# The first token group's output products in the seven-product scheme: a fused HGRN2 attention and maxout FFN kernel

## The chip, the cores and the metric
One core of one Trainium2 chip. The metric is the device time of one execution in microseconds (us); the median of three runs of the kernel before is 415.52 us (415.25 to 416.81). Beside the times there is one profiled execution, from which every duration below is taken.

## What is computed
An HGRN2 recurrence gives x, and a maxout FFN with three input matrices is applied to it, all in float32:

```python
f = 1 / (1 + exp(-f_logit))                       # q, k, v, f_logit: (4, 8, 768, 48)
for t in range(S):                                # S = 768
    state = f[:, :, t, :, None] * state + einsum('bhd,bhe->bhde', k[:, :, t], v[:, :, t])
    y[:, :, t] = einsum('bhd,bhde->bhe', q[:, :, t], state)
x = y.transpose(0, 2, 1, 3).reshape(3072, 384)
h = maximum(maximum(x @ w1, x @ w2), x @ w3)      # w1, w2, w3: 384 x 768
out = h @ w_out                                   # w_out: 768 x 384
```

## The kernel before, in words
**Units and groups.** The work is cut into 24 units (u = 0 to 23) of 128 tokens, which go through the recurrence, and into 6 groups (g = 0 to 5) of 4 units, which go through the FFN as blocks of 512 tokens. For a unit the program runs `sigmoids` (ACT), `scan` (DVE, L329), `after` (DVE turns k; GpSimd writes `ends` L339 and `kh` L340), `before` (DVE scan L347; GpSimd writes `qh` L351), `carry` (GpSimd, L357), `keys_by_blocks` (DVE transposes of `kh`, L382), `pairs` (PE, L392; it needs the unit's `kh` and `qh`), `values` and `sums` (PE, L411 and L436), and `finish` (PE L500, then three ACT copies L506 into xT). In the code `pack` then moves the rows of xT that lie in the wrong place, by two DMAs (L519). Units 0 to 5 are loaded by rows; from unit 6 (`BY_ROWS`) one `load` fetches two units by 24 DMAs (L183).

**The FFN.** The maximum is taken over differences: w1 is subtracted from w2 and w3 (`apart`, L745), the maximum with 0 of the two remaining products gives hm, and the part `x @ w1 @ w_out` is added back through a precomputed matrix `w_nat = w1 @ w_out` (`linear`, L772, nine matmul steps in three rows `a`). `place` (L450) rearranges w2 - w1, w3 - w1 and `w_nat` by ten DMAs each into `placed[0]`, `placed[1]` and `w_lin`, the order in which groups 1 to 5 hold x.

- Group 0 has a path of its own, `ffn_first` (L786): plain products (L537), rounding of the float64-typed weights as they arrive (`round_to`, L750), `linear`, and `outputs` (L557): for each of its four units nine matmuls of 128x384 into one bank, an ACT copy to `o`, and two stores.
- Groups 1 to 5 use a Strassen-like scheme of seven block products in place of eight. `inputs_by_pairs` (L858) makes hm; it needs sums of the weights (`mix_in`, L833, four GpSimd operations of 128x768 into `w_sum` and `placed[1]`) and of x (`sums_of_x`, L845, five GpSimd operations). `outputs_by_pairs` (L614) makes the outputs by matmuls of 128x192; it needs sums of hm (`sums_of_hm`, L605, four GpSimd operations of 128x256 for each of three j pairs) and differences of w_out and `w_lin` (`mix` L583, `mix_x` L589, on GpSimd). One PSUM bank `a` accumulates in several stages: after each stage ACT copies it out (`read`, L635) and the next product adds into the same bank.

**Order.** All engines' instructions run in program order (`manual_schedule`). The FFN is a Python generator that yields an estimated PE cost after each piece. The main loop (L1060) runs the steps of a unit and between them calls `fill(part)` (L956), which adds `part` to a budget and draws FFN pieces while the budget is above zero. With `part` = 2360 for u = 4 to 7 and 2432 after that, the program fixes which FFN piece stands between which unit steps, and `PART` (L976) is such that four units draw just the estimated cost of one group of the new scheme. The cost of the yields of one group therefore shifts every later FFN piece against the unit steps. `ffn(g)` is appended in the loop of unit 4g + 4, after `pack(3, 3)` of the group.

**Queues around the change.** SP issues loads, `place`, `pack` and stores one by one, about 0.63 us each. In program order it has: `load(8)` (24 DMAs, in the loop of u = 5), `v` of unit 7, `place` for `placed[0]`, `v` of unit 8, `place` for `placed[1]`, `place` for `w_lin`, `pack(0, 2)` of group 1, `load(10)`. GpSimd has, after the last rounded weight piece (L258): kh and qh of unit 7, its `carry`, the four `mix_in` with kh and qh of unit 8 between them, one `mix`, the steps of unit 9, `sums_of_x(1)`, and the other three `mix`. The buffers: `w_mix` lies in `w_in[2]`, `w_sum` in `placed[2]`, `s_mix` (sums of hm) in `w_in[1]`.

Of the kernel before, what the change touches and what calls it, by code (L numbers as in the profile page):

```python
# [55 lines left out]
def kernel(  # L56
# [33 lines left out]
    def fast():  # L90
        ctx = ExitStack()
        with ctx:
# [463 lines left out]

            def outputs(hm, xT, i):  # L557
                p = bank()
                t = slice(i % 2 * UT, (i % 2 + 1) * UT)
                terms = [(hm[:, j, i * UT:(i + 1) * UT], w_out[:, j, :]) for j in range(NJ)]  # L560
                terms += [(by_halves(xT)[:, i // 2, k, t], w_nat[:, k, :]) for k in range(NK)]
                for n, (lhsT, rhs) in enumerate(terms):
                    nc.tensor.matmul(p[:, 0:DM], lhsT=lhsT, rhs=rhs, start=(n == 0), stop=(n == NJ + NK - 1))  # L563
                    if n % NK == NK - 1:
                        if n == NJ + NK - 1:
                            o = o_four[:, i]
                            nc.scalar.copy(o, p[:, 0:DM])
                            store(i, o)
                        yield NK * DM * COLUMN

            HJ, HD = NJ // 2, DM // 2
            corner = lambda k, n: w_out[:, k::2, n * HD:(n + 1) * HD]
            w_mix = [corner(0, 1)] + [w_in[2][:, :, n * HD:(n + 1) * HD] for n in range(4)]
            x_mix = [w_lin[:, 0, HD:]] + [w_mix[4][:, n] for n in range(2)] + [keep.tile([128, HD], FP32, name="mix")]
# [4 lines left out]
            def mix(n):  # L583

                dst, x, y = ((w_mix[2], corner(1, 1), corner(0, 1)), (w_mix[0], corner(0, 1), corner(0, 0)),
                             (w_mix[1], corner(1, 1), w_mix[0]), (w_mix[3], corner(1, 0), w_mix[1]))[n]
                nc.gpsimd.tensor_tensor(dst, x, y, op=ALU.subtract)

# [16 lines left out]
            def sums_of_hm(hm, jj):  # L605
                sums_of_pair(hm[:, 2 * jj], hm[:, 2 * jj + 1], *(t[:, jj] for t in s_mix))
# [7 lines left out]
            def outputs_by_pairs(g, hm, xT):  # L614
                tile_of = lambda p, n: slice((2 * p + n) * UT, (2 * p + n + 1) * UT)
                half = lambda n: slice(n * HD, (n + 1) * HD)
                order = [*range(HJ - 1), HJ, HJ - 1]
                A = lambda k, n: lambda p: [(xT[:, k] if jj == HJ else hm[:, 2 * jj + k])[:, tile_of(p, n)] for jj in order]
# [3 lines left out]
                              for t, x in zip(s_mix, s_of_x(xT)))  # L622
                X = lambda n: lambda p: [xT[:, 2, tile_of(p, n)]]
                lin, lin_mix = [[w_lin[:, 2, half(n)]] for n in range(2)], [w_mix[4][:, 2]]
                partial = [w_nat[:, n, :] for n in range(NK)]
                last = g == NU // GRP - 1
# [16 lines left out]
                a, b, c = bank(), bank(True), bank(True)  # L643
                sums_of_x_pair(xT, 0)
                into(b, 0, X(0), lin[0])
# [4 lines left out]
                for p in range(2):  # L650
                    into(a, p, A(0, 0), C(0, 0), early)
                    if p:
                        sums_of_x_pair(xT, 1)
                    yield COST - PART_COST
                    into(b, p, A(1, 0), C(1, 0), early)
                    yield COST - PART_COST
# [129 lines left out]
            def ffn_first(xT):  # L786
# [4 lines left out]
                for j, t in steps:  # L791
                    w = t.stop - t.start
                    for i in (1, 2):
                        p = yield from product(xT, j, i, t)
                        if i == 1:
                            nc.scalar.copy(hm[:, j, t], p)
                        else:
                            nc.vector.scalar_tensor_tensor(hm[:, j, t], hm[:, j, t], 0.0, p, op0=ALU.max, op1=ALU.max)
                        round_to(ROUNDED[n_step])
                        load_weights(2, rounded[0] - 1)  # L800
                        yield (1 if w == TOK else NK) * w * COLUMN
                        n_step += 1
                        if n_step in TURNED:
                            yield from turn(TURNED[n_step])
                for a in range(NK):
                    if a < 2:
                        for n in range(2 * NK + 2):
                            place(placed[a].bitcast(FP32), w_in[a + 1], n)
                    for cost in linear(a):
                        round_to(rounded[0] + 1)  # L810
                        yield cost
                for n in range(2 * NK + 2):
                    place(w_lin, w_nat, n)
                made = iter([lambda n=n: mix_in(n) for n in range(4)] + [lambda: mix(0)])
                for i in range(GRP):
                    for n, cost in enumerate(outputs(hm, xT, i)):
                        if i or n:
                            next(made, lambda: None)()
                        if i == GRP - 1 and n == 1 and 1 in packed:
                            sums_of_x(1)  # L820
                        if i == GRP - 1 and n == 2:
                            for k in range(1, 4):
                                mix(k)
                        yield cost

# [4 lines left out]
            w_two = [t.bitcast(FP32) for t in placed[0:2]]  # L830
            w_sum = [placed[2].bitcast(FP32)[:, n] for n in range(NK)]

# [25 lines left out]
            def inputs_by_pairs(g, hm, xT):  # L858
# [57 lines left out]
                def fourth(n):  # L916
# [5 lines left out]
                    sums_of_hm(hm, n)  # L922
                    if g == 1:
                        for i in ((0, 1), (2, 3, 4), ())[n]:
                            mix_x(i)
                    yield COST
# [54 lines left out]
            with tc.manual_schedule():  # L981
# [78 lines left out]
                for u in range(GRP, NU):  # L1060
# [7 lines left out]
                    if u > GRP:  # L1068
                        finish(u - 1, xT)
                        if u % GRP == 3:  # L1070
                            pack(0, 2, xT)
                        elif u % GRP == 0:
                            pack(3, 3, xT)
                    if u % GRP == 0:
# [6 lines left out]
                    if u + 2 <= BY_ROWS:  # L1081
                        load(u + 2)
                    if BY_ROWS <= u + 3 < NU and u % 2:
                        load(u + 3, one, "fkq" if u % GRP == 1 else "f")
                    if u + 2 < NU:
                        load_v(u + 2)
                    keys_by_blocks(u, 3)
                    if n < NU:
                        if n < BY_ROWS:
                            sigmoids(n)  # L1090
                        if n != BY_ROWS:
                            scan(n)
# [6 lines left out]
                    if BY_ROWS < u + 2 < NU and u % GRP == 0:  # L1099
                        load(u + 2, one, "k")  # L1100
                    values(u)
                    if n < NU:
                        carry(n)
# [8 lines left out]
                    if u + 2 >= CHECKS:  # L1112
                        check_load(u + 2 - CHECKS)
                    if BY_ROWS <= u + 2 < NU:
                        sigmoids(u + 2)
# [272 lines left out]
```

## Time and profile before

| what | value |
|---|---|
| median of three runs | 415.52 us |
| the profiled execution's own time | 416.47 us |
| its span, first to last instruction | 414.6 us |
| TensorE (PE) busy | 397.8 us, 96% |
| GpSimd (POOL) busy | 245.2 us, 59% |
| VectorE (DVE) / ScalarE (ACT) busy | 290.8 us, 70% / 178.7 us, 43% |
| mean granted TensorE clock | 0.998 |
| PE: `linear` | 77.28 to 91.83 us |
| PE: `outputs` of group 0 | 91.83 to 120.12 us |
| PE: first product of groups 1, 2, 3, 4 | 120.12, 181.64, 241.26, 300.86 us |

A float32 matmul stands as two records in the trace, so the 36 matmuls of `outputs` are 72 records. The duration of a record contains the pipeline's depth; the pace is the distance from one start to the next. A line of the timeline gives the start, the duration, the engine, the line of the kernel, output and inputs, and, in brackets, the idle time before it with what ended it.

### The profile page before, as it was taken

Reading aid. Unit: us, or ns where it says so; the run is one execution under the profiler, and the core shown is the slowest. Engines: PE = TensorE matmul, PEld = TensorE weight load, DVE = VectorE, ACT = ScalarE, POOL = GpSimd, SP = SyncE. Lnnn points to the kernel's source line nnn. Section 1 sums busy time; section 2 is a strip of 40 time slices with the busy share of each in tenths; the row PEclk is TensorE's granted clock in tenths of the full one; section 3 lists DMA queues with packets and bytes.
Section 4 is the critical chain, followed back from the end, with each engine's and each line's share of the span. In section 5 each row is a group of like instructions: output and inputs, shape, how many; then the busy total and the mean of one; then the engine's idle time right before and its main releaser. Section 6 shows DMA issues by size and latency. Waiting matters only on the chain.

```text
span 414.6 us, 11546 instructions
## 1 busy us (share of the span) xinstructions
PE 397.8 (96%) x4598; PEld 332.4 (80%) x4598; DVE 290.8 (70%) x569; ACT 178.7 (43%) x412; POOL 245.2 (59%) x270
## 2 busy tenths in 40 slices
PE   4988999999999999999999999999999999999995
PEld 4766775566668889998889988889988899988984
DVE  6987897996695899898888976988894550002500
ACT  2478786511223531444541354533345324576210
POOL 2189694730989887487496376667466860435700
PEclk9999999999999999999999999999999999999999
DMA  8989987677356767377625376724473011541002
GB/s 170 237 261 273 250 231 93 86 143 159 83 104 96 122 114 132 70 118 89 137 78 104 52 117 86 163 64 80 71 146 96 2 55 44 148 136 60 0 21 62
DMA packets 181562, 47.21 MB, mean 114 GB/s; under 512 B 160448, under 2 KB 179200, under 8 KB 181504
## 3 DMA queue, kind: packets, MB, share of 16 engines
q1 hardware_dynamic: 178032, 45.62, 54.0%
q10 hardware_dynamic: 3472, 0.81, 0.9%
q8 instruction: 37, 0.61, 0.6%
q14 instruction: 21, 0.17, 0.1%
HBM read 37.75 MB, written 4.72 MB: 102 GB/s over the span
## 4 chain that ended last, share of the span: by engine, by line
PE 76%; DVE 6%; SPq 5%; POOL 3%; DMA 3%; ACT 3%; issue 2%; ACTq 0%; POOLq 0%; DVEq 0%
PE p L870 16%; PE p L631 14%; PE tr L870 13%; PE tr L631 11%; PE p L537 6%; PE p L563 3%; PE y L411 3%; PE y L500 2%; PE p L776 2%; SPq L174 2%; DMA raw<-in_moe_w_dram 2%; PE a L392 2%; PE y L436 2%; DVE ks L382 2%; SPq L164 1%
## 5 line engine op out<-in xcount | busy, mean ns | idle before, releaser
L382 DVE STREAM_TRANSPOSE ks<-kh 32x128 f32<-32x128 f32 x256 | 77.4, 302 | 11.9 <-POOL kh L340 7.7
L870 PE MATMUL tr<-xT,placed 128*128 128x256 f32 x300 | 72.6, 385 | 0.3 <-DVE hm L913 0.3
L870 PEld LDWEIGHTS tr<-xT,placed 128*128 128x128 f32 x300 | 55.7, 190 | 9.3 <-ACT hm L878 1.2
L870 PE MATMUL p<-xT,placed 128*128 128x256 f32 x180 | 45.1, 382 | 0.3 <-POOL xT L854 0.3
L339 POOL COPY ends<-r 128x8 f32<-128x8 f32 x24 | 9.8, 407 | 48.5 <-DVE r L329 48.5
L870 PEld LDWEIGHTS p<-xT,placed 128*128 128x128 f32 x180 | 33.7, 190 | 5.3 <-POOL xT L854 0.7
L537 PE MATMUL p<-xT,w_in 128*128 128x256 f32 (+1 forms) x108 | 33.9, 458 | 3.0 <-POOL w_in L745 2.2
L329 DVE TENSOR_TENSOR_SCAN r<-gate,from_one 128x520 f32<-128x520 f32 x24 | 31.5, 1314 | 6.1 <-ACT gate L308 3.0
L340 POOL TENSOR_TENSOR kh<-kt,r 128x512 f32<-128x512 f32 x18 | 30.1, 1671 | 7.6 <-DVE kt L296 6.2
L639 DVE TENSOR_TENSOR o<-tr,w_in 128x384 f32<-128x384 f32 (+1 forms) x11 | 5.7, 521 | 38.6 <-PE tr L631 35.1
L347 DVE TENSOR_TENSOR_SCAN prod<-gate,from_inv 128x520 f32<-128x520 f32 x24 | 32.1, 1336 | 0.0
L603 POOL TENSOR_TENSOR w_in<-hm 128x256 f32<-128x256 f32 x15 | 11.1, 739 | 34.9 <-DVE hm L921 32.2
L506 ACT COPY xT<-y 64x256 f32<-64x256 f32 (+1 forms) x60 | 22.1, 369 | 19.2 <-PE y L500 18.1
L870 PE MATMUL p<-w_in,placed 128*128 128x256 f32 x120 | 30.0, 379 | 0.0
L913 DVE TENSOR_TENSOR hm<-tr,hm 128x512 f32<-128x512 f32 x15 | 10.3, 688 | 26.6 <-PE tr L870 19.7
L537 PEld LDWEIGHTS p<-xT,w_in 128*128 128x128 f32 x108 | 19.5, 190 | 11.8 <-issue 6.0
L636 ACT COPY w_in<-p 128x384 f32<-128x384 f32 x15 | 7.2, 478 | 46.0 <-PE p L631 46.0
L631 PE MATMUL p<-w_in,hm 128*128 128x192 f32 x120 | 25.4, 335 | 1.1 <-ACT w_in L636 1.1
L258 POOL TENSOR_TENSOR w_in<-top_bits,rest_bits 128x384 uint32<-128x384 uint32 x18 | 21.8, 1218 | 7.6 <-DVE top_bits L252 4.7
L280 ACT ACTIVATE raw<-top_bits 128x384 f32<-128x384 f32 x48 | 25.2, 526 | 0.4
L870 PEld LDWEIGHTS p<-w_in,placed 128*128 128x128 f32 x120 | 22.8, 190 | 3.1
L631 PE MATMUL tr<-w_out,w_in 128*128 128x192 f32 x120 | 24.4, 326 | 0.0
(159 smaller groups left out, 907.6 us busy)
## 6 DMA issues: line engine op xcount, KB each, us to landing
raw<-in_moe_w_dram SPq DMA_DIRECT2D x24, 384.0 KB, 3.8
v_ld<-in_v_dram SPq DMA_DIRECT2D x48, 96.0 KB, 3.2
placed<-in_moe_w_dram SPq DMA_DIRECT2D x12, 384.0 KB, 5.4
out_dram<-o SPq DMA_DIRECT2D x46, 96.0 KB, 2.2
placed<-in_moe_w_out_dram SPq DMA_DIRECT2D x6, 384.0 KB, 6.3
f_ld<-in_f_logit_dram SPq DMA_DIRECT2D x36, 64.0 KB, 3.4
k_ld<-in_k_dram SPq DMA_DIRECT2D x36, 64.0 KB, 2.5
q_ld<-in_q_dram SPq DMA_DIRECT2D x36, 64.0 KB, 2.5
```

The costliest lines, as they stand in the source:

```text
L258: nc.gpsimd.tensor_tensor(dst, by(top), by(rest), op=ALU.add)
L280: nc.scalar.activation(over, size, AF.Relu, scale=(-1 / HI_MIN, 1.0)[step - 1], bias=(1.0, -HI_END * (1 - 2.0 ** -24))[step - 1], accum_ou ...
L329: nc.vector.tensor_tensor_scan(r[:, 0:LEN][:, ::-1], flat(gate)[:, ::-1], flat(from_one)[:, ::-1], 1.0, op0=ALU.mult, op1=ALU.max)
L340: (nc.vector if u < BY_ROWS else nc.gpsimd).tensor_tensor(kh.rearrange("p h a t -> p a h t"), kt, by_batch(r[:, 1:LEN + 1].rearrange("p (x ...
L347: nc.vector.tensor_tensor_scan(flat(prod), flat(gate_tiles[u % 2]), flat(from_inv[u % 2]), 1.0, op0=ALU.mult, op1=ALU.max)
L382: nc.vector.transpose(ks[n * 32:(n + 1) * 32, :, par, e0:e0 + 32], kh[p0:p0 + 32, :, a, t0:t0 + 32])
L411: nc.tensor.matmul(y[o:o + DP, a, hp * C:(hp + 1) * C], lhsT=v_ld[s, 2 * hp + par, :], rhs=d["at"][s, par, hp, :], start=(hp == 0), stop=F ...
L506: nc.scalar.copy(xT[o, :, t0 + a * C:t0 + (a + 1) * C], y[i, a, 0:HP * C].rearrange("p (h t) -> p h t", h=HP))
L537: nc.tensor.matmul(p if w < TOK else p.rearrange("p (two t) -> p two t", two=2), lhsT=w_in[i][:, kt, j * 128:(j + 1) * 128], rhs=x[:, t.st ...
L563: nc.tensor.matmul(p[:, 0:DM], lhsT=lhsT, rhs=rhs, start=(n == 0), stop=(n == NJ + NK - 1))
L631: nc.tensor.matmul(b[:, p * HD:(p + 1) * HD], lhsT=x, rhs=w, start=id(b) not in begun, stop=True, skip_group_check=True)
L870: nc.tensor.matmul(b[:, j * HALF:(j + 1) * HALF], lhsT=w[:, (2 * n + j) * 128:(2 * n + j + 1) * 128], rhs=x, start=begin and j == 0, stop= ...
```

## The change
`ffn_first` now calls `outputs_by_pairs(0, hm, xT)` in place of four `outputs`. For group 0 (`mixed` false) x is not part of the seven-product scheme: it enters through plain products with `w_nat`, three matmuls for each half where the later groups have one, and `order` has three entries instead of four. Partial sums go to `rests` instead of `w_nat`.

Other steps move. Both `place` calls for the input weights stand ahead of `linear`, and `load(8)` moves from the loop of u = 5 to that of u = 6, in two parts (f after `pairs`, k and q after `values`), with `sigmoids(8)` moved to the loop of u = 7. `mix(0)` to `mix(2)` stand in `linear`'s first row, the twelve operations of `sums_of_hm` in its second, `mix(3)` and the new `mix(4)` behind it, the four `mix_in` with the first four pieces of the outputs, `mix_x` behind them. `w_mix` and `w_sum` trade places in memory. The stores of group 0 come later, out of `store_late` in group 1. `pack` of group 1 goes to ACT's queue.

```diff
-            w_mix = [corner(0, 1)] + [w_in[2][:, :, n * HD:(n + 1) * HD] for n in range(4)]
+            spare = placed[2].bitcast(FP32).rearrange("q k c -> q (k c)")
+            w_mix = [corner(0, 1)] + [spare[:, n * NK * HD:(n + 1) * NK * HD].rearrange("q (k c) -> q k c", k=NK)
+                                      for n in range(4)]
...
-                dst, x, y = ((w_mix[2], corner(1, 1), corner(0, 1)), (w_mix[0], corner(0, 1), corner(0, 0)),
-                             (w_mix[1], corner(1, 1), w_mix[0]), (w_mix[3], corner(1, 0), w_mix[1]))[n]
-                nc.gpsimd.tensor_tensor(dst, x, y, op=ALU.subtract)
+                dst, x, y = ((w_mix[2], corner(1, 1), corner(0, 1)), (w_mix[1], w_mix[2], corner(0, 0)),
+                             (w_mix[3], corner(1, 0), w_mix[1]), (w_mix[0], corner(0, 1), corner(0, 0)),
+                             (w_mix[4], w_nat[:, :, 0:HD], w_nat[:, :, HD:]))[n]
+                nc.gpsimd.tensor_tensor(dst, x, y, op=ALU.add if n == 1 else ALU.subtract)
...
-                order = [*range(HJ - 1), HJ, HJ - 1]
+                mixed = g > 0
+                order = [*range(HJ - 1), *[HJ] * mixed, HJ - 1]
...
+                else:
+                    X = lambda n: lambda p: [by_halves(xT)[:, p, k, n * UT:(n + 1) * UT] for k in range(NK)]
+                    lin = [[w_nat[:, k, half(n)] for k in range(NK)] for n in range(2)]
+                    lin_mix = [w_mix[4][:, k] for k in range(NK)]
+                    partial = [rests[:, 0], rests[:, 1], rests[:, 0]]
...
+                for a in range(2):
+                    for n in range(2 * NK + 2):
+                        place(placed[a].bitcast(FP32), w_in[a + 1], n)
                 for a in range(NK):
-                    if a < 2:
-                        for n in range(2 * NK + 2):
-                            place(placed[a].bitcast(FP32), w_in[a + 1], n)
-                    for cost in linear(a):
-                        round_to(rounded[0] + 1)
+                    for n, cost in enumerate(linear(a)):
+                        round_to(len(pieces))
+                        if a == 0:
+                            mix(n)
+                        elif a == 1:
+                            sums_of_hm(hm, n)
                         yield cost
                 for n in range(2 * NK + 2):
                     place(w_lin, w_nat, n)
-                made = iter([lambda n=n: mix_in(n) for n in range(4)] + [lambda: mix(0)])
-                for i in range(GRP):
-                    for n, cost in enumerate(outputs(hm, xT, i)):
...
+                mix(3)
+                mix(4)
+                for n, cost in enumerate(outputs_by_pairs(0, hm, xT)):
+                    if n < 4:
+                        mix_in(n)
+                    yield cost
+                for m in range(5):
+                    mix_x(m)
...
-            w_sum = [placed[2].bitcast(FP32)[:, n] for n in range(NK)]
+            w_sum = [w_in[2][:, n] for n in range(NK)]
...
-                    if g == 1:
-                        for i in ((0, 1), (2, 3, 4), ())[n]:
-                            mix_x(i)
...
+                        queues = act if u <= 2 * GRP else one
...
-                            pack(0, 2, xT)
+                            pack(0, 2, xT, queues)
                         elif u % GRP == 0:
-                            pack(3, 3, xT)
+                            pack(3, 3, xT, queues)
...
-                    if BY_ROWS <= u + 3 < NU and u % 2:
-                        load(u + 3, one, "fkq" if u % GRP == 1 else "f")
-                    if u + 2 < NU:
+                    if u == BY_ROWS:
+                        load(u + 2, one, "f")
+                    elif u + 1 != BY_ROWS:
+                        if BY_ROWS <= u + 3 < NU and u % 2:
+                            load(u + 3, one, "fkq" if u % GRP == 1 else "f")
+                    if u + 2 < NU and u != BY_ROWS:
                         load_v(u + 2)
...
-                        if n < BY_ROWS:
+                        if n < BY_ROWS or n == BY_ROWS + 2:
                             sigmoids(n)
...
+                    if u == BY_ROWS:
+                        load(u + 2, one, "kq")
+                        load_v(u + 2)
...
-                    if BY_ROWS <= u + 2 < NU:
+                    if BY_ROWS <= u + 2 < NU and u != BY_ROWS:
                         sigmoids(u + 2)
```

## The prediction
> **What bounds the kernel now.** I read the page first: PE is busy 397.8 of 414.6 us, at full clock in all slices but for the start.
>
> ```profile
> PE 397.8 (96%) x4598; PEld 332.4 (80%) x4598; DVE 290.8 (70%) x569; ACT 178.7 (43%) x412; POOL 245.2 (59%) x270
> ...
> PE   4988999999999999999999999999999999999995
> ...
> POOL 2189694730989887487496376667466860435700
> ```
>
> From 77 us on PE hardly stops, so the end moves by the PE work that goes, less each gap that comes. The second view is PE's timeline: where do gaps arise? At the very end, where no unit steps are left, ACT's copy of bank `a` stands open between two products into that bank. First the end of group 5's second stage, then the same place in group 1:
>
> ```profile
> 398.39 0.49 PE L631 MATMUL p<-w_in,w_in 128*128 128x192 f32 x2
> 399.44 0.92 PE L631 MATMUL p<-w_in,hm 128*128 128x192 f32 x4 [0.57 <-ACT w_in L636]
> ...
> 168.80 0.49 PE L631 MATMUL p<-w_in,w_in 128*128 128x192 f32 x2
> 169.22 0.66 PE L500 MATMUL y<-qh,state 48*48 48x64 f32 x32
> 169.81 0.69 PE L392 MATMUL a<-qh,kh 48*64 48x64 f32 x32
> 170.44 0.92 PE L631 MATMUL p<-w_in,hm 128*128 128x192 f32 x4
> ```
>
> Two records issue in 0.325, so at 398.39 the next could start at 398.72; it starts at 399.44: **0.72 us lost**. At 168.80 the same copy costs nothing, as `finish` and `pairs` of a unit stand in between. The third view is GpSimd's timeline around group 0's outputs (PE 91.83 to 120.12):
>
> ```profile
> 81.02 1.00 POOL L258 TENSOR_TENSOR w_out<-top_bits,rest_bits 128x384 uint32<-128x384 uint32 x1 [0.88 <-DVE top_bits L254]
> ...
> 87.18 1.96 POOL L340 TENSOR_TENSOR kh<-kt,r 128x512 f32<-128x512 f32 x1 [0.71 <-DVE kt L296]
> ...
> 104.15 1.81 POOL L839 TENSOR_TENSOR placed<-placed 128x768 f32<-128x768 f32 x1 [13.09 <-DMA w_in<-w_in]
> ...
> 106.06 1.19 POOL L340 TENSOR_TENSOR kh<-kt,r 128x512 f32<-128x512 f32 x1
> 107.21 1.18 POOL L351 TENSOR_TENSOR qh<-qt,prod 128x512 f32<-128x512 f32 x1
> ...
> 114.45 2.34 POOL L587 TENSOR_TENSOR w_in<-w_out 128x576 f32<-128x576 f32 x1
> ...
> 128.83 1.41 POOL L587 TENSOR_TENSOR w_in<-w_out 128x576 f32<-128x576 f32 x1
> ```
>
> GpSimd idles 13.09 us for `place`'s DMAs, and qh of unit 8 ends at 108.39, just ahead of its `pairs` on PE at 108.49. The same operation takes 1.19 or 1.96, and 1.41 or 2.34: the long ones lie over a DVE scan (prod from 86.96, r from 113.86). A scan costs GpSimd about 0.8.
>
> **The change part by part.** The terms are against this execution (416.47 us, span 414.6), 0.95 above the median; I carry their sum to 415.52.
>
> *1. PE work of group 0.* Before: 36 matmuls of 384 columns, 72 records; six undisturbed ones (96.96 to 98.89) give 0.322 each, 23.2 us. After: eleven stages of six 192-column matmuls, 66 or 132 records at 0.1625 (20 in 3.25 in the chain of waits), 21.45; smaller pieces add some 0.1. Saved 1.8 to 2.6 (the upper by L563's whole stretches, 24.0); I take **-1.9**, since restarts after unit steps are nearly as many.
> The Trainium skill, "TensorE: Matmul & The Clock Gate", Back-to-back issue gap, gives N/2.4 + 2.5 ns for an isolated matmul. As an estimate with two passes a record that is 0.325 and 0.165, and the saving 1.6: the rule charges short matmuls more than the rows do.
>
> *2. GpSimd's queue from 82.02 us.* After the last L258 (ends 82.02) the program now has, without a gap: `mix` 0 to 2, one `sums_of_hm`, ends, kh, qh of unit 7, two `sums_of_hm`, `carry`, **`mix(3)`**, `mix(4)`, four `mix_in`, ends, kh, **qh of unit 8**. From start to start uncontended: mix 1.4 to 1.45, four sums 2.85 (L603, 141.37 to 144.22), ends+kh+qh 2.45, carry 0.78, mix_in 1.79. So: 82.0 + 4.35 + 2.85 + 2.45 + 5.7 + 0.8 = 98.15, `mix(3)` to 99.6, `mix(4)` to 101.0, `mix_in` to 108.1, qh(8) to 110.6 at the earliest. Under this unbroken queue lie DVE's scans r(7), prod(7) (84.97, 86.96 now), r(8), prod(8): three by `mix(3)`, four by qh(8), +2.4 and +3.2. I take 102.0 and 113.8.
> "GPSIMD Engine Reference", section 3.1 of the Trainium skill, puts a two-input operation at 2.6 cycles of 1.2 GHz per element. As an estimate the queue's 11,456 elements are 24.8 us, qh(8) would end at 106.9 and the second wait below vanish. That lacks each operation's start and the scans; the rows decide.
>
> PE's demand: lin ends at 91.83; two stages 1.95, finish and pairs (7) and a restart to 94.92 as now; then six pieces of 0.65 to **98.9**, where the first seven-product stage (`c`, s1 by `w_mix[0]`) needs `mix(3)`: wait 102.0 - 98.9 = **+3.1** (0.7 without scans). On to `pairs(8)`: 0.975, values 1.08, 2.05, 0.975, the uncovered copy of `a` (below) **+0.7**, three pieces 2.9, finish 0.5: 9.1 in all, 111.1; qh(8) is there at 113.9: **+2.8** (1.9 without scans). Behind the waiting matmuls stands all of PE's queue; DVE and ACT wait for PE later, so nothing is won beside. Sum for group 0: -1.9 + 3.1 + 0.7 + 2.8 = +4.7.
>
> *3. Queues.* `place` (20 x 0.63) starts on SP where `load(8)` started: 72.2, its last lands near 87, long before `mix_in`. `load(8)` then issues 84.9 to 90 (f) and to 99.4 (k, q), landing near 102; DVE turns q(8) at 101.6 now, and qh(8) is stuck in GpSimd's queue until 112: covered; if GpSimd were early, at most 1 us. `pack` passes to ACT: two issues of 0.70 (L519 on ACT, 349.27) ahead of sig(8), which ends near 98 where DVE is still on unit 7's transposes: nothing. Eight stores leave SP's stretch of 117 to 134, so k, q of unit 10 and x of group 1 come earlier. Now DVE waits 3.5 and 1.5 for them, GpSimd 1.9 for `pack`. PE's stretch of group 1 is 61.5 (120.12 to 181.64) against 59.6 for groups 2 and 3, so at most 1.9 returns, at least nothing as GpSimd comes late; I take **-1.4**. The removed `mix` and `mix_x` of group 1 lie in the same 1.9.
>
> *4. The shifted budget.* Group 0's yields fall from 23.04 to 21.12 us, so by the program's own sums every later FFN piece stands 1.92 earlier among the unit steps. I went through the budget yield by yield; for the present kernel this gives the timeline's order. In the new order the second stage's copy and the next product into `a` come in one `fill` in groups 0 to 4; `finish` and `pairs` come only after that product. ACT's copy (0.48 and two semaphores) then stands open: 0.72 each in groups 1 to 4 and the 0.7 above. The third copy loses `values` as cover: 0.08 (403.45 to 403.53 in group 5), about 0.5 in group 4 where ACT has `pack` and checks ahead of it. In return `sixth` and `fifth` part (-0.09 a group). Three times 0.71 and once 1.13: **+3.3**. The x sums on DVE come as close as 0.4 us ahead of their matmul; bound 0 to 0.3 a group, I take 0.
>
> Total: 4.7 - 1.4 + 3.3 = **+6.6**, 415.5 + 6.6 = **422.1 us**. Its own bounds: no scan contention, all 1.9 back, group 4 without the 0.5: -1.9 + 0.7 + 0.7 + 1.9 - 1.9 + 2.8 = +2.3, 417.8; nothing back, scans at 0.95, x sums late: +9.7, 425.2.
>
> **The rivals.**
> *GpSimd keeps up* (the other side: not slower). If `w_mix[0]` is there by 98.9 and qh(8) by 108.0, both waits go. For: 13 us of idle time lie in this stretch now. Against: the bare minimum of the rows is already 99.6 and 110.6. Price: -1.9 + 0.7 - 1.4 + 3.3 = +0.7, 416.2.
> *The copies stay covered.* If unit steps stand between copy and product, 0.7 and 3.3 go: -1.9 + 3.1 + 2.8 - 1.4 = +2.6, 418.1. Against: the budget decides, and a yield of 1.28 against a balance of 0.83 is not close.
> *Both*, and the change does just what it is arranged for: -1.9 - 1.4 = -3.3, 412.2.
> *It doesn't begin as early as it says*: if `mix(3)`, in place in w_out, holds up all products with w_out behind it and not `w_mix[0]` alone, PE waits at 95.1 already; 102.0 + 13 = 115 against 113.9 at `pairs(8)`: +1.1, 423.2. Nothing in the trace tells.
>
> **How the numbers follow.** Forecast 0.55, GpSimd keeps up 0.13, copies covered 0.10, both 0.14, earlier wait 0.08. A measurement tells 0.5% (2.1 us) from no change. Faster by more: 0.14 (both). Same: 0.13 of keeping up less 0.02 for its upper end, and 0.04 of copies covered: 0.15. Slower: 0.71. The range leaves out "both" and a little above 425: 414.5 to 425.2.
>
> **What would show it.** PE: gaps ahead of L631 put down to POOL L587 near 99 and ahead of L392 to POOL L351 near 111; one gap of 0.6 to 0.7 at each group's A01 product put down to ACT L636; group starts shifted by +4.7, then 0.7 a group. GpSimd: no idle time from 82 to 113. It is wrong if group 1 starts before 120 us, or if `finish` stands between copy and product.

## The result and the profile after

The changed kernel takes **427.52 us** (median of 4 runs, 426.21 to 429.69), the kernel before in the same series 415.88 (415.25 to 416.81): ratio 1.028 [1.0235, 1.0332], slower by some 11.6 us. The forecast was 422.1 with a range up to 425.2: the direction held, the size did not. The profiled execution took 426.21 us with a span of 424.3.

From the page of the changed kernel, PE's share, its slices and its clock:

```profile
PE 399.3 (94%) x4658; PEld 342.3 (81%) x4658; DVE 295.4 (70%) x571; ACT 179.0 (42%) x413; POOL 254.5 (60%) x284
...
PE   4988999997699999999999999999999999999995
...
PEclk9999999998899999999999999999999999999999
```

The two weak slices of PE, 7 and 6, are 95 to 117 us; there the clock drops as well, which it does in no slice of before:

```profile
PEclk9999999999999999999999999999999999999999
```

So I cut PE's timeline of each kernel at the first product of the linear stage and at the first product of each group (us):

| stretch | before | changed | e1 | e3 | e9 |
|---|---|---|---|---|---|
| linear stage and group 0's outputs | 42.84 | 51.52 | 47.87 | 47.93 | 42.08 |
| group 1's stretch | 61.52 | 60.49 | 60.46 | 59.50 | 59.72 |
| group 2's | 59.62 | 60.48 | 60.47 | 59.61 | 59.62 |
| group 3's | 59.60 | 60.47 | 60.46 | 59.62 | 59.61 |
| group 4's | 57.81 | 58.60 | 58.70 | 57.82 | 57.81 |
| group 5's, to the end of the span | 55.93 | 55.95 | 56.1 | 57.1 | 56.0 |

(e1, e3, e9 are experiments below; e3's last stretch has 1.1 us more behind the last product, where the last stores land.) Group 0 pays 8.7 us in the profiled execution, the fastest of the four; forecast was 4.7. Group 1 wins 1.0 in all; groups 2 to 4 pay 0.8 to 0.9 each. PE's timeline of the changed kernel has these gaps in group 0 (start, duration, engine, line, operation; in brackets the idle time ahead and who ended it):

```profile
101.03 1.97 PE L623 MATMUL tr<-w_out,w_in 128*128 128x192 f32 x6 [2.23 <-POOL w_out L572]
...
108.61 3.69 PE L623 MATMUL p<-placed,w_in 128*128 128x192 f32 x12 [2.55 <-ACT rest_bits L628]
112.87 2.22 PE L623 MATMUL p<-placed,hm 128*128 128x192 f32 x12 [0.57 <-ACT rest_bits L628]
...
117.09 0.67 PE L500 MATMUL y<-qh,state 48*48 48x64 f32 x32 [1.03 <-DVE st L444]
```

The first is the forecast wait for `mix(3)`, the third the uncovered copy of `a`. The second and the fourth are new. The fourth is late by the same cause as the second: `st` stands on DVE behind the turning of q(8), which waits 2.20 us for q of unit 8 to land. At 108.61 PE waits for `read(a, 0)`, an ACT copy of 0.46 us. Why is it late? ACT's timeline:

```profile
95.08 1.40 ACTq L519 DMA_DIRECT2D xT<-xT  x2
107.56 0.63 ACT L311 ACTIVATE sig<-f_ld 128x512 f32<-128x512 f32 x1 [12.12 <-DMA f_ld<-in_f_logit_dram]
108.10 0.46 ACT L628 COPY rest_bits<-p 128x384 f32<-128x384 f32 x1
```

The copy stands behind sig(8), and sig(8) waits 12.12 us for unit 8's f. SP issues that load only at 99.78. SP's timeline:

```profile
79.83 19.85 SPq L461 DMA_DIRECT2D placed<-w_in  x8
99.78 4.29 SPq L183 DMA_DIRECT2D f_ld<-in_f_logit_dram  x8
```

Eight issues of `place` take 19.85 us, since one stands. In before the same eight took 5.04:

```profile
96.84 5.04 SPq L461 DMA_DIRECT2D placed<-w_in  x8
```

SP's waits of the changed kernel in the same stretch (us in total, times, longest):

```profile
SPq L461 <- DMA xT<-xT: 13.8, 1, 13.8
```

`xT<-xT` is the `pack(0, 2)` that this kernel issues on ACT. Why should a `place` wait for it? In the built program every DMA of SP and of ACT reports its landing on one of eight completion semaphores, taken in turn by both queues, and waits first for the DMA that used that number before. SP's ten DMAs of the second `place`, with the number that each takes:

```
L454 placed<-w_in  DMAHW4
L454 placed<-w_in  DMAHW7
L461 placed<-w_in  DMAHW0, 1, 2, 3, 4
L461 placed<-w_in  DMAHW5
L461 placed<-w_in  DMAHW6
L461 placed<-w_in  DMAHW7
```

Between the first and the second, `pack(0, 2)` took 5 and 6. So the eighth and ninth wait until it has landed, and it waits for ACT's copies (94.30) of what PE's `finish(6)` gives at 93.6. SP's order is strict, and all of unit 8's loads stand behind. The Trainium skill, "DMA: Bandwidth & Descriptors", section "Why a DMA increments its semaphore by 16 and not by 1", says why such a wait has to be there: two DMAs in flight on one semaphore can't be told apart. In this trace the wait takes 13.8 us of SP.

### The profile page after: what moved, and what is told of

Its sections match the earlier page's. It is cut to its first block, busy times and chain, and to the rows that moved or that the text cites. A ratio compares the mean times of both kernels' runs of the same rounds, so it can differ in the third digit from the quotient of the medians.

```text
span 424.3 us, 11681 instructions
## 1 busy us (share of the span) xinstructions
PE 399.3 (94%) x4658; PEld 342.3 (81%) x4658; DVE 295.4 (70%) x571; ACT 179.0 (42%) x413; POOL 254.5 (60%) x284
## 4 chain that ended last, share of the span: by engine, by line
PE 82%; SPq 4%; DVE 3%; issue 2%; DMA 2%; POOL 2%; ACT 2%; ACTq 0%; DVEq 0%; POOLq 0%
PE p L864 19%; PE tr L864 16%; PE p L623 16%; PE tr L623 12%; PE p L537 5%; SPq L183 3%; PE y L500 3%; PE y L411 3%; PE a L392 2%; PE p L769 2%; PE y L436 2%; SPq L461 1%; POOL w_in L258 1%; PE y L407 1%; PE tr L291 1%
## 5 line engine op out<-in xcount | busy, mean ns | idle before, releaser
L864 PE MATMUL tr<-xT,placed 128*128 128x256 f32 x180 | 43.7, 379 | 0.0
L864 PEld LDWEIGHTS tr<-xT,placed 128*128 128x128 f32 x180 | 34.2, 190 | 4.6
L623 PE MATMUL p<-placed,hm 128*128 128x192 f32 x144 | 30.9, 337 | 4.1 <-ACT w_in L628 3.6
L623 PE MATMUL tr<-w_out,w_in 128*128 128x192 f32 x144 | 29.7, 334 | 2.2 <-POOL w_out L572 2.2
L864 PE MATMUL tr<-xT,w_in 128*128 128x256 f32 x120 | 31.7, 387 | 0.0
L685 POOL TENSOR_TENSOR o<-top_bits,w_in 128x384 f32<-128x384 f32 x5 | 5.1, 1016 | 43.5 <-ACT w_in L628 43.5
L864 PE MATMUL p<-xT,placed 128*128 128x256 f32 x120 | 29.6, 383 | 0.0
L623 PEld LDWEIGHTS p<-placed,hm 128*128 128x128 f32 x144 | 23.6, 190 | 7.3 <-ACT w_in L628 6.2
L623 PEld LDWEIGHTS tr<-w_out,w_in 128*128 128x128 f32 x144 | 24.7, 193 | 2.6 <-POOL w_out L572 2.5
L588 POOL TENSOR_TENSOR w_in<-hm 128x256 f32<-128x256 f32 x18 | 14.0, 780 | 21.0 <-DVE hm L915 21.0
```

The source lines that it names most:

```text
L588: engine.tensor_tensor(dst, x, y, op=op)
L623: nc.tensor.matmul(b[:, p * HD:(p + 1) * HD], lhsT=x, rhs=w, start=id(b) not in begun, stop=True, skip_group_check=True)
L864: nc.tensor.matmul(b[:, j * HALF:(j + 1) * HALF], lhsT=w[:, (2 * n + j) * 128:(2 * n + j + 1) * 128], rhs=x, start=begin and j == 0, stop= ...
```

## The experiments

Theory after the result: (a) that wait of SP costs what group 0 has above its forecast; (b) the rest is as forecast, GpSimd's queue and the uncovered copies, and behind each long gap a slow clock comes on top. Rivals: ScalarE itself is what `pack` delays; the slow clock is an independent cost; the shift harms by late inputs, not by copies.

**e1: both packs back on SP**, the changed kernel otherwise.

```diff
-                        queues = act if u <= 2 * GRP else one
+                        queues = one
```

> Group 1's two pack steps go back from ACT's queue to SP's; all else is the changed kernel. Theory 1 (ordering between the two DMA queues): the trace of the changed kernel shows SP stuck for 13.8 us in the second place (84.1 to 97.9), put down to the landing of pack's DMA, which ACT issues after PE's finish of unit 6. With pack on SP that wait goes; unit 8's f is issued near 85 to 90 instead of 99.8 to 104, ACT's sig(8) ends near 98 instead of 108.2, and PE's wait ahead of the second-stage product (2.55 us, read put down to ACT) goes. What stays: the wait for mix(3) near 99 (2 to 3 us), slow records after it, and about 0.7 us at the copy of bank a in each group. Sum: 3 to 5 us faster than the changed kernel, 422 to 425 us. Rival A (place waits for its buffers: the raw weights or the differences in w_in): the 14 us gap in place stays and the time stays at 427. Rival B (GpSimd's queue alone sets group 0): the gap goes, but qh of unit 8 is late all the same, and the time falls by less than 1.5 us.

422.82 us (422.52 to 423.45), ratio 1.0177 [1.0154, 1.02]: 4.7 us of the change's loss. Its timelines of SP, then of PE:

```profile
79.24 5.57 SPq L461 DMA_DIRECT2D placed<-w_in  x8
84.91 4.29 SPq L183 DMA_DIRECT2D f_ld<-in_f_logit_dram  x8
```

```profile
102.04 1.47 PE L623 MATMUL tr<-w_out,w_in 128*128 128x192 f32 x6 [3.17 <-POOL w_out L572]
109.57 2.22 PE L623 MATMUL p<-placed,hm 128*128 128x192 f32 x12 [0.57 <-ACT rest_bits L628]
113.95 0.69 PE L392 MATMUL a<-qh,kh 48*64 48x64 f32 x32 [0.60 <-POOL qh L351]
```

The loads go out at 84.91, as forecast, and the gaps are the three forecast ones. Only the last is 0.60 instead of 2.8, though qh(8) ends at 113.90 as forecast (113.8): PE came there late. The windows of e1 say why (each row: stretch, its length, busy time and instructions of PE, PEld, DVE, ACT and POOL, then PE's granted clock, DMA share, GB/s):

```profile
102.00:104.00 2.00, 1.96 (x26) 1.52 (x30) 2.00 (x3) 0.00 (x0) 2.00 (x1) 0.73 0.39 106
104.00:106.00 2.00, 2.00 (x58) 1.91 (x51) 0.57 (x2) 0.00 (x0) 2.00 (x2) 0.50 0.31 78
```

Behind the gap of 3.17 us the clock is at 0.50 for some 3.4 us (0.27 x 2 / 0.5 = 1.1 in the first window, 2.0 in the second, the rest in the next), and products of 192 columns take up to twice as long. Half the clock for 3.4 us takes 1.7 us of PE work (an estimate).

**e2: the old budget** in the changed kernel, one charged stage without work.

```diff
                 for m in range(5):
                     mix_x(m)
+                yield NK * DM * COLUMN
```

> The changed kernel with one more yield of 1.92 us of estimated cost and no work behind it, at the end of group 0's outputs, so that all pieces of groups 1 to 5 stand among the unit steps as in the kernel before. Theory (the shifted budget uncovers the copy of bank a): the gap of 0.73 us ahead of the second-stage product goes in groups 1 to 3, and in group 4, so 2.5 to 3 us faster than the changed kernel (424.5 to 425). Group 0 is as in the changed kernel. Rival (the gaps are taken up elsewhere, for the unit steps then stand later against DVE and GpSimd): within 1 us of the changed kernel.

424.37 us (423.33 to 426.27), ratio 1.0202 [1.0176, 1.0228]: 3.15 less than the changed kernel. Its groups 1 to 4 take 59.51, 59.60, 59.62 and 57.72, together 3.6 less than in the changed kernel. But its group 0 is not "as in the changed kernel": it takes 54.43 for 51.52 in the profiled execution (the slowest of the four, 426.27). PE waits there 3.43 us for `st`, and the clock is at 0.50 from 117.2 to 124.0. What the budget is worth is therefore read from the groups behind it.

**e3: both.**

> Both edits: pack on SP and the additional yield. If the two causes are apart, their gains add: 6 to 8 us faster than the changed kernel, 419.5 to 421.5 us, that is still 4 to 5 us slower than the kernel before for the wait for mix(3) and the slow records behind it. If they share a cause, clearly less than the sum.

420.85 us (419.88 to 421.21), ratio 1.0121 [1.0095, 1.0146]: 6.7 less, against 4.7 and 3.15 alone; the 1.2 missing to their sum is well inside the 3.5 us over which the changed kernel's own four runs spread. What is left is group 0. e3 is the base of the runs from e5 on.

**e4: the kernel before, with the new budget.**

```diff
-                        yield NK * DM * COLUMN
+                        yield NK * DM * COLUMN * 11 / 12
```

> The kernel before with the yields of group 0's outputs cut from 23.04 to 21.12 us and nothing else: the same instructions, but the pieces of groups 1 to 5 in the places that they have in the changed kernel. If the budget's shift alone uncovers the copies: 2.5 to 3.5 us slower than the kernel before, 418 to 419 us, with gaps of 0.7 us put down to ACT L636 in groups 1 to 4. Rival: no gaps of this kind, no change within 1 us.

424.18 us (422.91 to 425.23), ratio 1.0203 [1.0171, 1.0236]: 8.4 more where 2.5 to 3.5 was expected. Groups 2 to 4 pay 60.46, 60.47 and 58.69, as expected. The miss is group 1, 65.91 for 61.52. PE's timeline there:

```profile
124.90 1.13 PE L870 MATMUL p<-xT,placed 128*128 128x256 f32 x4 [1.71 <-POOL xT L854]
139.90 1.99 PE L870 MATMUL tr<-xT,placed 128*128 128x256 f32 x8 [0.98 <-DVE hm L913]
```

In before the same two waits are 0.30 and 0.34 us. The difference makes 2.05 of the 4.4 us that group 1 loses; the uncovered copy (0.57) and three smaller waits (0.86, 0.35, 0.24) stand in the rest. In the old order the sums of x come so late that the product pulled forward waits for them. So here the shift has two prices; the changed kernel does not show the second (its group 1 takes 60.49).

**e5: the clock.** On e3, seven products nobody uses fill the wait for `mix(3)`.

```diff
+                for _ in range(0 if mixed else 7):
+                    nc.tensor.matmul(c[:, 0:256], lhsT=ident, rhs=from_one.rearrange("p x t -> p (x t)")[:, 0:256],
+                                     start=True, stop=True)
                 into(c, 0, s1, T(0))
```

> Base: e3_pack_sp_old_budget, 420.85 us. Added: seven products of 256 columns ahead of the first seven-product stage of group 0, into a bank that is overwritten at once, so that TensorE computes through most of the 3.21 us in which it waited for mix(3) and its clock stays up; their results are used by nobody. Theory (the granted clock fell because of that wait, but the end of group 0 is set by qh(8) on GpSimd, which ended at 114.62 in e3): the clock is 1.0 behind the wait, the 2 us that the slow clock cost come back as a wait at pairs(8), 0.56 us grows to 2 to 2.7, and the time stays within 0.7 us of e3: 420 to 421.5 us. Rival A (the slow clock is itself a cost): 1.5 to 2 us less than e3, 419 us, and no longer wait at pairs(8). Rival B (the clock does not follow the gap): the clock stays at 0.5 to 0.6 and nothing changes.

420.55 us (418.87 to 421.08), ratio 1.0089 [1.0069, 1.0109]; 0.3 from e3. (Before stood 0.4 us higher in the series of e5 to e8 than in that of e1 to e4, and 0.65 higher in that of e9 to e12; a difference across series is no surer than that.) PE's timeline of e5, then its windows:

```profile
102.12 1.24 PE L623 MATMUL tr<-w_out,w_in 128*128 128x192 f32 x6 [0.20 <-POOL w_out L572]
...
114.04 0.69 PE L392 MATMUL a<-qh,kh 48*64 48x64 f32 x32 [2.11 <-POOL qh L351]
```

```profile
102.00:104.00 2.00, 1.88 (x54) 1.65 (x56) 2.00 (x3) 0.00 (x0) 2.00 (x2) 1.00 0.45 123
114.00:116.00 2.00, 1.96 (x37) 1.90 (x38) 1.92 (x7) 0.00 (x0) 0.77 (x1) 0.72 0.64 97
116.00:118.00 2.00, 2.00 (x8) 2.00 (x7) 1.90 (x6) 0.48 (x1) 0.59 (x1) 0.50 0.30 63
```

As the theory says: at full clock PE comes to `pairs(8)` early and waits 2.11 us for the same qh(8). What it did not say: this gap then has its own slow clock. Rival A, 1.5 to 2 us, falls by the wait of 2.11. The time alone would not tell: two of the six executions, with a mean clock of 0.999 and 1.000, took 418.87 and 419.03, the four with 0.991 to 0.996 took 420.52 to 421.08, so the second slow clock seems to strike in some executions and not in others.

**e6: `mix_in` behind qh(8)** in GpSimd's queue, and **e7: e5 and e6 together.**

```diff
-                    if n < 4:
-                        mix_in(n)
+                    if 10 <= n < 14:
+                        mix_in(n - 10)
```

> Base: e3_pack_sp_old_budget, 420.85 us. Moved: the four mix_in operations (7.2 us on GpSimd) from the first four stages of group 0 to its stages 10 to 13, so that the built order has kh(8) and qh(8) ahead of them. Theory: the wait at pairs(8), 0.56 us, goes; the wait for mix(3) (3.21 us) and the slow clock stay: 0.5 to 1 us less than e3, 420 us, if the sums now last in the queue do not delay group 1. Rival (what stands behind qh(8) in the queue is late instead, the sums of group 1's inputs): as e3 or up to 2 us more, with a wait for xT sums or w_in at the start of group 1.

419.99 us (419.50 to 420.70), ratio 1.0085 [1.0068, 1.0102], 0.9 under e3, but group 0's stretch is no shorter (48.20): the wait at `pairs(8)` is gone, and behind the first gap (3.19) the clock stays at 0.50 from 102 to 108.

> Both edits, on e3_pack_sp_old_budget (420.85 us). Theory: now neither qh(8) nor the slow clock holds group 0, and what is left of its cost is the wait for mix(3): 2 to 2.7 us less than e3, 418 to 419 us, clearly more than the sum of the two edits alone (0.5 to 1 and 0). Rival A of the first run (the slow clock is a cost by itself): the gains of the two edits just add up. If the sums in the back of the queue are late, up to 2 us of it is lost.

416.81 us (416.32 to 417.43), ratio 1.0019 [1.0007, 1.0031]: 4.0 under e3, where 0.3 and 0.9 came from the two alone. The clock is 1.00 in every window of group 0 and no wait but the copy's 0.57 exceeds 0.2 us. More than expected (2 to 2.7): taking away either gap leaves a slow clock behind the other.

**e8: two of three sums on VectorE.**

```diff
-                            sums_of_hm(hm, n)
+                            sums_of_pair(hm[:, 2 * n], hm[:, 2 * n + 1], *(t[:, n] for t in s_mix),
+                                         engine=nc.vector if n else nc.gpsimd)
```

> Base: e3_pack_sp_old_budget, 420.85 us. The sums of the second and third pair of hidden rows (8 operations, 5.7 us of GpSimd's queue) go to VectorE. Theory (the length of GpSimd's queue is what group 0 pays for): mix(3) ends near 97 instead of 102.69, before TensorE asks for it at 99.5, so that wait, the slow clock and the wait at pairs(8) all go: 4 to 5 us less than e3, 416 to 417 us, 0 to 1 above the kernel before. Rival (VectorE takes them late, behind its scans, or slows GpSimd): the wait moves to VectorE's sums, 1 to 3 us less, 418 to 420 us, with w_in by VectorE as the releaser.

417.37 us (415.89 to 420.38), ratio 1.0032 [1.001, 1.0055]: 3.5 under e3, between theory and rival. GpSimd's waits are gone; a new one came. DVE's timeline, then PE's:

```profile
88.42 0.38 DVE L588 TENSOR_TENSOR w_in<-hm 128x256 f32<-128x256 f32 x1
...
92.99 1.40 DVE L588 TENSOR_TENSOR hm<-hm 128x256 f32<-128x256 f32 x1
...
95.28 0.55 DVE L444 TENSOR_TENSOR st<-y,state 128x384 f32<-128x384 f32 x1
```

```profile
95.88 0.66 PE L500 MATMUL y<-qh,state 48*48 48x64 f32 x32 [2.37 <-DVE st L444]
```

The eight sums stand ahead of the state `st` on DVE, and PE's `finish(6)` waits for that, again with a clock of 0.50 behind it (98 to 100).

**e9: the same queue in another order.** On e3, the back half of the second and third sums goes behind `mix(3)`, `mix_in` behind qh(8) as in e6; nothing added, nothing removed.

```diff
-                            sums_of_hm(hm, n)
+                            sums_of_pair(hm[:, 2 * n], hm[:, 2 * n + 1], *(t[:, n] for t in s_mix),
+                                         part=slice(0, 2 if n else 4))
...
                 mix(3)
+                for n in (1, 2):
+                    sums_of_pair(hm[:, 2 * n], hm[:, 2 * n + 1], *(t[:, n] for t in s_mix), part=slice(2, 4))
                 mix(4)
```

> Base: e3_pack_sp_old_budget (420.85 us), without fillers. GpSimd's queue only re-ordered, no operation added or removed: the third and fourth operation of the second and third pair's sums (four of 0.73 us) go behind mix(3), and mix_in behind qh(8) as in e6. Theory: mix(3) ends 2.9 us earlier, near 99.8, when TensorE asks for it at 99.5, so that the wait (3.21 us) falls under 0.5 us, the clock stays up, and nothing waits at pairs(8): e7_fill_late less its seven fillers (3.0 us), 413.8 us (413.3 to 414.5), below the kernel before (416.2). Rival (fillers kept the clock up that a shorter wait would not; or the moved operations are late for the later stages): 415.5 to 418 us, with a wait at a later stage of group 0 or a granted clock under 0.8 behind a gap of under 1 us.

**413.99 us** (413.29 to 414.75), ratio 0.9949 [0.9931, 0.9967]: 2.4 under before, 13.5 under the changed kernel, and where the theory put it. GpSimd's `mix(3)`, then PE's stages:

```profile
96.84 1.40 POOL L572 TENSOR_TENSOR w_out<-w_out 128x576 f32<-128x576 f32 x1
```

```profile
98.60 1.14 PE L623 MATMUL tr<-w_out,w_in 128*128 128x192 f32 x6
...
104.50 2.22 PE L623 MATMUL p<-placed,hm 128*128 128x192 f32 x12 [0.57 <-ACT rest_bits L628]
```

`mix(3)` ends at 98.24, 0.36 us before PE comes for it. Counted from the start of the linear stage (76.76, in e3 77.52) that is 3.7 us earlier than in e3, not 2.9, as `carry` ahead of it no longer lies over a DVE scan (0.83 for 1.76).

**e10: the copy in group 0 covered** by the two stages into bank `c`, on e9.

```diff
                 read(a, 1)
                 yield COST
+                if not mixed:
+                    into(c, 0, X(0), lin[1])
...
+                    into(d, 1, X(0), lin[1])
...
                 into(a, 0, A(0, 1), T(2))
```

> As e9_reordered, and in group 0 the two stages into the third bank go between the copy of the first bank and its next use, so that the copy (0.57 us idle in each profile so far) is covered. Theory: 0.5 to 0.6 us less than e9, 413.2 us, and no idle time in front of the third seven-product stage. Rival: the later read of that bank by the add is late, and the time stays as in e9.

413.74 us (413.41 to 414.69), ratio 0.9938 [0.9922, 0.9954]: not to be told from e9. PE's timeline shows the wait at the next copy of the same bank, which had those two stages as its cover:

```profile
111.73 2.22 PE L623 MATMUL p<-placed,hm 128*128 128x192 f32 x12 [0.62 <-ACT rest_bits L628]
```

**e11: e10 with the changed kernel's budget.**

> As e10_reordered_swap, but with the changed kernel's own budget (the shift by one charged stage). Theory: the uncovered copies of groups 1 to 4 come back, 0.57 us idle in each group, and it takes 2 to 3 us more than e10: 415.2 to 416.2 us, about the kernel before. Rival (with the start of group 1 earlier than in e1, its inputs are late, as in e4_before_new_budget): 5 to 7 us more than e10, with waits for the sums of xT in group 1.

417.47 us (417.0 to 418.67), ratio 1.0032 [1.002, 1.0044]: 3.7 more than e10, a little over the 2 to 3 expected. Groups 1 to 4 have the 0.57 again, group 4 a second gap of 0.82 at its next copy. Group 1 pays most, 61.06 for e10's 59.51, but its only other wait is 0.29 us for an ACT copy: its sums of x are not late, so e4's second price belongs to the old kernel's queues.

**e12: only `pack(3, 3)` on ACT**, the changed kernel otherwise.

```diff
-                        queues = act if u <= 2 * GRP else one
+                        queues = act if u == 2 * GRP else one
```

> Base: the changed kernel (427.52 us; with both packs of stage 0 on SP 422.82 us). Only pack(0, 2) goes back to SP; pack(3, 3), one unit later, stays on ScalarE's queue. Theory (SP's second placement stands because its seventh and eighth transfer wait for completion numbers that pack(0, 2) took): this is the whole of it, SP's placement runs unbroken, and the time is that of e1_pack_on_sp, 422.5 to 423.5 us. Rival A (packs on ScalarE's queue cost by delaying ScalarE, each its share): between, 424.5 to 426 us. Rival B (pack(3, 3) is the one that costs): 427 us.

423.96 us (423.35 to 424.39), ratio 1.0182 [1.0162, 1.0202]: 3.6 of the 4.7 us are back, 1.1 above e1 and half a microsecond outside the theory's span. Of the 1.1, before's own rise between the two series makes 0.65; by their ratios to before e12 and e1 (1.0177) can't be told apart. The second `place` runs unbroken; the same wait now stands in the third. SP's waits, then its timeline, in e12:

```profile
SPq L461 <- DMA xT<-xT: 6.6, 1, 6.6
```

```profile
103.00 12.12 SPq L461 DMA_DIRECT2D w_in<-w_in  x8
```

So the wait follows the pack that is on ACT, and its price depends on what stands behind it: here loads of later units, for which nothing waits in group 0. In the profiles the two differ in group 0 (49.53 for e1's 47.87), and that goes with the clock; PE's timeline, then the windows:

```profile
101.88 1.24 PE L623 MATMUL tr<-w_out,w_in 128*128 128x192 f32 x6 [3.22 <-POOL w_out L572]
...
113.80 0.89 PE L392 MATMUL a<-qh,kh 48*64 48x64 f32 x32 [2.12 <-POOL qh L351]
```

```profile
102.00:104.00 2.00, 2.00 (x70) 1.77 (x70) 1.97 (x3) 0.00 (x0) 2.00 (x1) 1.00 0.65 146
114.00:116.00 2.00, 2.00 (x36) 1.88 (x30) 1.92 (x7) 0.00 (x0) 0.53 (x1) 0.53 0.18 47
```

The same gap of 3.2 us that slowed e1's clock leaves it at 1.00 here; the second gap slows it, and nothing hides that one. Why is worked out below.

## Why the prediction was wrong in size

- **Step 3, Queues: the step that failed.** "`pack` passes to ACT: ... nothing." I weighed its two issues on ACT and not what they do to SP. Undoing it is worth 4.7 us by the medians (e1; 3.65 in group 0 of the two profiles), and with it the forecast would have stood: 422.82 for 422.1. "`load(8)` then issues 84.9 ... covered" is right in e1 (84.91) and 15 us off in the changed kernel (99.78), where sig(8), gate(8) and qh(8) are late one behind the other. That the price comes through the shared numbers and not through ACT's own time is shown by SP's wait of 13.8 us, put down to `pack`'s own DMA, and by e12: with one pack still on ACT the time can't be told from e1's, and the wait moves to another `place`.
- **Step 2, the wait for `mix(3)`, +3.1.** 3.17 in e1, with `mix(3)` ending at 101.99 (forecast 102.0); 2.23 in the changed kernel, where late loads keep the scans away. That it goes by order alone (e9) shows that GpSimd's queue was the cause.
- **Step 2, the wait at `pairs(8)`, +2.8.** qh(8) ended at 113.90 in e1 (forecast 113.8). The wait was 0.60 there and 2.1 in e5 and e12: the slow clock behind the first gap ate it. I had no term for the clock. In sum it hardly matters in e1 (group 0 +5.0 for +4.7), since qh(8)'s end sets the time either way.
- **Step 1, PE work, -1.9.** e9's group 0 has no gap but the copy's and is 0.76 shorter than before's; with 0.7 for the copy that is -1.5. The term was too large: by its own rows the lower end is 23.2 - 21.45 - 0.1 = 1.65, not 1.8, and the other estimate beside it, 1.6, was nearer than the 1.9 taken.
- **Step 3, group 1, -1.4.** 61.52 became 59.50 with the old budget (e3): -2.0, the whole of the stretch that I had bounded at 1.9.
- **Step 4, the shifted budget, +3.3.** e1 less e3 by stretches: 0.96 + 0.86 + 0.84 + 0.88 = 3.5; by medians 2.0, 3.15 (e2) and 3.7 (e11 less e10). Place and mechanism as forecast.
- **The rivals.** "GpSimd keeps up" and "the copies stay covered" fall with the lines above. "Both", 412.2 us, is about what e9 and e10 reach, once order and budget are mended: 414. The earlier wait on all of w_out did not occur: in e1 the products up to 98.9 ran through. The range ended at 425.2 since all its cases left the queues at no cost.

**When a gap slows the clock.** Gaps of 2.11 (e5), 2.12 (e12's second), 2.23, 2.37 (e8), 2.55, 3.17, 3.2 and 3.43 us (e2) were followed by a clock of 0.50. e12's first, 3.22, was not, nor were 1.80 (e2) and 1.71 (e4), nor any of about 0.6. Length alone doesn't decide. Short windows of the changed kernel show when its clock switches:

```profile
101.20:101.40 0.20, 0.20 (x2) 0.20 (x3) 0.00 (x0) 0.00 (x0) 0.20 (x1) 0.97 1.00 153
104.60:104.80 0.20, 0.20 (x12) 0.12 (x7) 0.00 (x0) 0.00 (x0) 0.20 (x1) 0.50 0.70 108
104.80:105.00 0.20, 0.20 (x5) 0.19 (x2) 0.00 (x0) 0.00 (x0) 0.20 (x1) 1.00 1.08 146
108.20:108.40 0.20, 0.00 (x0) 0.00 (x0) 0.18 (x1) 0.20 (x1) 0.20 (x1) 0.54 0.54 76
111.60:111.80 0.20, 0.20 (x2) 0.20 (x2) 0.20 (x1) 0.00 (x0) 0.00 (x0) 0.93 0.80 120
```

A mean of 0.97 over 0.2 us is full clock but for the last 0.01. So the clock goes down at 101.39, up at 104.80, down at 108.22 and up at 111.63, each time 3.41 us later. In e2 it goes down at 103.50, up at 106.91, down at 117.16 and up at 123.98: 1, 4 and 6 times 3.41 us after the first. Within one execution the switches stand on a grid of 3.41 us, and each slow stretch between 25 and 360 us lasts 3.4 or 6.8 us. Laid over that grid, the gaps sort themselves:

| run | window of the grid, us | PE idle in it, us | clock after it |
|---|---|---|---|
| e3 | 99.42 to 102.83 | 3.21 | 0.50 |
| e1 | 99.51 to 102.92 | 2.53 | 0.50 |
| e8 | 93.53 to 96.95 | 2.35 | 0.50 |
| e2 | 113.74 to 117.16 | 2.30 | 0.50 |
| changed | 97.98 to 101.39 | 2.23 | 0.50 |
| changed | 104.80 to 108.22 | 2.16 | 0.50 |
| e12 | 110.72 to 114.13 | 2.12 | 0.50 |
| e5, e6 | 111.47 to 114.89, 97.97 to 101.38 | 2.11 each | 0.50 |
| e2 | 100.09 to 103.50 | 1.90 | 0.50 |
| e12 | 97.07 to 100.48 | 1.82 | 1.00 |
| e2 | 106.91 to 110.33 | 1.80 | 1.00 |
| e12 | 100.48 to 103.89 | 1.40 | 1.00 |

So between 25 and 360 us of all these profiles the clock halved after every window in which PE idled 1.90 us or more, and after none with 1.82 or less. e12's first gap was cut in two by the border of a window, and cost only itself. The slow stretch doubled to 6.8 us where the next window held over 1 us of waiting too (1.08 in e6, 1.13 in e2). The Trainium skill, "TensorE: Matmul & The Clock Gate", Part 1, has the clock halve after an idle window of some 3.4 us that runs freely, whatever the kernel does. The grid agrees with that; but the window need not be idle throughout, since 1.90 us in it was enough here.

**What stays open.** Where between 1.82 and 1.90 us the border lies, and whether it is the same elsewhere: each kernel has one profiled execution, and no run here was built to move a gap over the grid.

## What to carry to other kernels

Moving DMAs to an idle queue is not free when queues share completion numbers in turn: count on to the next DMA with the same number (here eight on), and ask whether it may wait for the moved one. When a slow engine's queue becomes unbroken, first order it by who is waited for: e9 moved nothing to another engine and was 3.4 us under e8, which did. Price a gap of about 2 us or more on PE at the gap and, if it falls into one window of the clock's grid, at 1.7 us of PE work on top (3.4 where the clock stays low for two windows; both are estimates from half the clock over 3.4 and 6.8 us). Mend all such gaps of a stretch at once, since mending one brings little (0.3 us in e5, 0.9 in e6) while another catches the same time.

## What the hardware showed beside

- VectorE and GpSimd slow each other; forecast was only that scans slow GpSimd. In e8, beside DVE's sums, GpSimd's own took 0.90 us for 0.73 in e3 and its kh 1.36 for 1.18. The scan r took DVE 1.24 us at 97.84 of before, where GpSimd idles, and 1.73 at 113.86 beside a `mix`. DVE's sums in e8 took 0.38 to 1.40 us; how much of that is GpSimd's doing is not shown, since no run has them with GpSimd idle.
- In the profiles the time from the last product to the end of the span, in which the last stores land, is 5.0 us in before and e9 but 6.1 in e3 and 6.5 in e10; spans that differ by 1 us say nothing about the stretches, which is why these were compared.
